# A new instruction order for a one-core attention and PReLU kernel: every step at a new place, fill matmuls regrouped, alpha's loads behind a GpSimd step

## The chip, the cores and the metric

The kernel runs on one core of a Trainium2 chip. A core has a matrix engine (TensorE, "PE" in the profile; its weight loads are listed apart as "PEld"), a vector engine (VectorE, "DVE"), an activation engine (ScalarE, "ACT"), a general engine (GpSimd, "POOL") and a queue engine (SyncE, "SP"). Each engine runs its own list of instructions in order; engines wait for one another through semaphores. A DMA (a copy between main memory and the core's memory SBUF, or a transposing copy) is issued as an instruction of SP, ACT or POOL and runs beside the engines once issued. TensorE writes into PSUM, eight banks of 2 KB per partition that VectorE and ScalarE read out.

The metric is the device time of one execution in microseconds (us), the median of several runs.

## The reference, cut to what matters

There are eight batches of eight heads, 512 tokens of width 64, and 32 states per head. Tokens read the states and the states read the tokens, both through a softmax; what was read goes, heads joined to a row of 512, through a two-layer network with a PReLU whose slope `alpha` differs for each of the 2048 hidden columns.

```python
scores = x @ state.T / 8                     # per batch and head
xread  = softmax(scores, over states) @ state        # (512, 64)
sread  = softmax(scores.T, over tokens) @ x          # (32, 64)
rows   = heads joined of concat([xread, sread])      # (8 * 544, 512)
h = rows @ w_in                                      # (4352, 2048)
g = maximum(h, 0) + alpha * minimum(h, 0)
out = g @ w_out                                      # (4352, 512)
```

## The kernel before, in words

**An order written out.** The kernel's steps are small functions. A string `ORDER` (line 18) names them one after the other with their arguments, and the loop at line 767 calls them in that order, under a manual schedule: nothing is reordered afterwards. So the order of the string is the order of the instructions on each engine and each queue; semaphores for true dependences and for the reuse of buffers are put in by the framework. A token is `step.arguments`. The last argument, where it is a letter, is the engine that does the copy: `a` ScalarE, `v` VectorE, `p` GpSimd.

**Stages.** For each batch b the steps are:

- `lx` (line 160) loads x of the batch in 16 bits by a DMA that POOL issues, into one of three buffers `xg`; `xd` (291) issues on SP the transposing DMA that writes `xT`. Batches 0 and 1 are transposed on TensorE instead (`xt` 299, with the copy `xo` 304), and batch 0 is loaded on SP in 32 bits and cast (`cx` 176), so that it can start early. The states come by `lst` (203), and are transposed on TensorE (`stt`, `sto`, `sbd`, `str`, `sro`, lines 244 to 282).
- `sc` (314) makes the scores, into a pair of PSUM banks called `two` of which there is one. From it follow two softmaxes. Over the states: `sb` (346, VectorE transposes 32x32 blocks), `smax` (379), `ssh` (384), `sexp` (393, ScalarE), `ssum` (402), `snorm` (406), `wb` (414, transposes back into `aT`). Over the tokens: `tm` (426), `nb` (433), `te` (443, ScalarE), `tsum` (453), `tn` (459 or 461), `tt` (465, a transposing DMA on SP into `e2T`). For batch 0 the state softmax works on scores of its own (`tsc` 353, in two halves) and `at`/`ao` (365, 368) transposes back on TensorE.
- `m` (507) multiplies the states by a quarter f of `w_in`, which makes the weights of the first layer directly from the states (the attention and `w_in` are one matrix then); `mo` (531, 533) copies the result to SBUF.
- `F` (556) is the first layer for one of 16 groups of 128 hidden columns: two matmuls into one bank, 512 tokens wide. `N` (609, ScalarE) takes the negative part out of that bank, `G` (612, VectorE) joins both to g; only then is the bank free. In batch 0 some of these come by halves of the tokens: `f`, `n`, `g` (578, 593, 597).
- In batch 0 `S` (626) is the second layer, in eight steps of two matmuls for each quarter of the tokens, and `O` (644) its output. From batch 1 on the second layer is done by seven products of half blocks instead of eight (a Winograd form of Strassen's scheme): `W` (670, GpSimd) makes differences of `w_out` once, `U` (694, GpSimd) makes sums and differences of g, `P` (715) are the products, four matmuls each, into the banks `px`, `py`, `pv`; `K` (731) keeps intermediate sums in SBUF, and `Q` (746, 748) makes and stores one quarter of the output, by an addition on VectorE or a copy on ScalarE, and a DMA on SP. Its buffer `osb` exists four times.
- `rd` (480) reads the tokens by the states' softmax, 32 small matmuls from `xg` and `e2T`; `rdo` copies the result. What all batches' states read is "batch 8", run at the end: its `F` is line 565.

**Weights.** `wi` (212) and `wo` (218) load quarters of `w_in` and `w_out` through POOL, with a cast. As POOL issues these DMAs itself, each is also 0.7 to 1.0 us of POOL's time. `W`, `U`, `tn` on POOL, `lx` and `lst` stand in the same queue.

**Fills.** `Z.k.n` (236) are n matmuls of a pattern into bank k which nobody reads; the setup does sixteen of them at the very start (`fill(0, 16)`).

**Banks.** Six banks are given out by number: the last digit of an `F`, and of the first `S` or `P` of a bank, is the bank 0 to 5 it takes. A step that takes a bank waits until its former content was read.

**alpha.** Before the loop the setup clears `alpha_rows` on VectorE (line 186) and issues its four loads on SP (188), behind the two loads of batch 0's x. `oma` (272, 273) turns it by a VectorE transpose and makes 1 - alpha on ScalarE, which every `G` and `g` needs.

Of the kernel before, what the change touches and what calls it, by code (L numbers as in the profile page):

```python
# [18 lines left out]
Z.0.3 stc.a stt.0 cx.0.1.v xt.0.0.1.1 xo.0.0.1.a wi.0 cx.0.0.v xt.0.0.0.2 xo.0.0.0.a sbd.0.v lst sbd.1.v Z.3.2 sto.a  # L19
Z.3.2 Z.3.3 cx.1.0.v xt.0.1.0.3 cx.1.1.v tsc.0.1.4 tsc.0.0 smax.0.0 ssh.v.0.0 xo.0.1.0.a xt.0.1.1.5 xo.0.1.1.a Z.1.3  # L20
Z.1.2 sc.0.0 sc.0.1 tsc.1.1.1 m.0.0.2.0 tsc.1.0 sexp.0.0 tm.0 smax.0.1 ssum.0.0 Z.3.3 mo.0.0.a.1 lx.1 Z.3.2 Z.3.2
Z.3.3 ssh.v.0.1 str.1.3 nb.0.a te.0.1 Z.5.3 str.0.5 Z.4.3 Z.4.3 te.0.0 sexp.0.1 Z.4.2 mo.0.0.v.0 Z.4.3 wi.1 ssum.0.1
wo.0 sro.0.a xt.1.0.0.4 snorm.p.0.0 at.0.0 ao.0.a wo.1 Z.1.3 tsum.0 snorm.p.0.1 xt.1.0.1.1 m.1.0 xt.1.1.0.2 sro.1.a
wi.2 oma.a xo.1.0.0.v wi.3 xo.1.0.1.v xo.1.1.0.a f.0.0.0.5 xt.1.1.1.0 n.0.0.0 mo.1.0.v at.1.4 ao.1.v m.0.1.1.3
tn.0.1.p mo.0.1.v.1 m.1.1 mo.1.1.a g.0.0.0.0 g.0.0.0.1 f.0.0.1.2 n.0.0.1 f.0.1.1.4 mo.0.1.a.0 n.0.1.1 f.0.1.0.3
xo.1.1.1.v g.0.0.1.1 g.0.0.1.0 sc.1 tm.1 m.2.0.5.0 mo.2.0.a.1 mo.2.0.a.0 F.0.5.1 N.0.5 F.0.4.2 N.0.4 nb.1.a te.1.1
g.0.1.1.0 g.0.1.1.1 G.0.5 S.0.3.0.0 wo.2 G.0.4 S.0.1.0.5 S.0.1.1 sb.1 F.0.7.4 N.0.7 G.0.7 F.0.6.1 wo.3 tn.0.0.p N.0.6
S.0.3.1 G.0.6 n.0.1.0 g.0.1.0.0 S.0.2.2.2 S.0.3.2 te.1.0 S.0.1.2 S.0.2.0 g.0.1.0.1 m.0.2 S.0.2.3 S.0.1.3 smax.1
mo.0.2.a F.0.8.4 N.0.8 G.0.8 W.1.1.p F.0.11.1 N.0.11 G.0.11 tsum.1 F.0.10.3 N.0.10 m.0.3 mo.0.3.a W.1.0.p lx.2 S.0.2.1
S.0.3.3 F.0.9.4 m.1.2 F.0.12.1 ssh.p.1 sexp.1 G.0.10 S.0.2.5 S.0.1.5 ssum.1.s N.0.9 G.0.9 F.0.13.3 S.0.3.5 mo.1.2.a  # L30
m.1.3 N.0.12 G.0.12 S.0.3.4 F.0.15.4 tn.1.1.a N.0.13 G.0.13 F.0.14.1 S.0.1.4 S.0.3.6 S.0.1.6 W.2.0.p S.0.2.4 N.0.15
snorm.p.1 wb.1 F.1.3.3 G.0.15 S.0.2.6 F.1.7.4 tn.1.0.a W.2.1.p N.0.14 G.0.14 mo.1.3.a N.1.3 G.1.3 N.1.7 G.1.7 xd.2
tt.0 S.0.3.7 O.0.3.a F.1.12.1 N.1.12 G.1.12 F.1.1.3 N.1.1 W.4.1.p F.1.9.0 G.1.1 N.1.9 G.1.9 tt.1 S.0.2.7 O.0.2.a
F.1.2.4 N.1.2 G.1.2 F.1.10.1 N.1.10 S.0.1.7 sc.2 O.0.1.a tm.2 sb.2 m.2.2.3.2 mo.2.2.a.0 W.4.0.p rd.0.0 G.1.10
mo.2.2.a.1 F.1.0.4 N.1.0 rdo.0.a W.3.1.p lx.3 S.0.0.6.5 nb.2.a F.1.8.3 N.1.8 G.1.0 smax.2 te.2.0 F.1.4.2 S.0.0.7 G.1.8
te.2.1 F.1.5.0 N.1.5 S.0.0.5 G.1.5 F.1.11.1 N.1.11 S.0.0.2 S.0.0.4 S.0.0.3 G.1.11 N.1.4 G.1.4 m.2.1 mo.2.1.a F.1.6.4
N.1.6 G.1.6 F.1.15.3 N.1.15 G.1.15 F.1.13.0 N.1.13 S.0.0.0 F.1.14.1 N.1.14 W.3.0.p S.0.0.1 O.0.0.a ssh.p.2 sexp.2 xd.3
U.1.1.0.p G.1.13 P.1.1.0.1.2 P.1.1.1.1 m.3.2 m.2.3.4.3 mo.2.3.a.1 mo.2.3.a.0 G.1.14 m.3.0.5.0 ssum.2.1 P.1.1.0.0
U.1.2.0.p mo.3.0.a.0 P.1.1.1.0 K.1.1.a P.1.2.0.0.3 snorm.v.2 wb.2 P.1.2.1.0 P.1.2.0.1 U.1.1.1.p U.1.2.1.p P.1.2.1.1
mo.3.2.a P.1.6.1.0 mo.3.0.a.1 m.3.3.4.5 mo.3.3.a.1 mo.3.3.a.0 rd.1.1 Q.1.0.0 sc.3 tm.3 m.4.0.0.5 mo.4.0.a.0 sb.3  # L40
P.1.6.0.0 mo.4.0.a.1 rdo.1.a F.2.6.4 N.2.6 G.2.6 F.2.13.3 N.2.13 P.1.6.0.1 P.1.6.1.1 F.2.0.0 F.2.12.5 F.2.8.1 G.2.13
K.1.2.a P.1.5.1.0 N.2.0 N.2.12 G.2.12 G.2.0 P.1.5.1.1 P.1.5.0.0 N.2.8 G.2.8 nb.3.a te.3.0 F.2.2.4 N.2.2 G.2.2 te.3.1
# [12 lines left out]
F.3.11.0 N.3.11 P.2.3.0.1 G.3.11 F.3.5.5 N.3.5 P.2.3.1.1 U.3.3.0.p P.2.3.0.0 G.3.5 mo.5.3.a.1 sexp.4 U.3.1.1.p
m.7.0.3.0 sc.5 P.2.3.1.0 Q.2.0.1.a mo.7.0.a.1 mo.7.0.a.0 tm.5 P.2.2.1.0.2 ssum.4.5 P.2.2.0.1 P.2.2.0.0 m.7.3.4.0
mo.7.3.a.1 mo.7.3.a.0 P.2.4.0.1 P.3.2.0.0.3 P.2.2.1.1 nb.5.a te.5.1 te.5.0 P.2.4.1.0 P.2.4.0.0 P.3.2.1.0 P.2.4.1.1
tsum.4 tn.4.0.a tn.4.1.a tt.4 P.3.2.0.1 snorm.v.4 wb.4 F.4.11.0 N.4.11 F.4.13.4 P.3.1.0.0.5 P.3.1.0.1 Q.2.1.0 sb.5
G.4.11 Q.2.0.0 xd.6 P.3.1.1.1 N.4.13 G.4.13 F.4.4.1 N.4.4 U.3.1.0.p G.4.4 U.3.2.0.p P.3.2.1.1 P.3.1.1.0 smax.5 K.3.1.a
Q.3.0.0 F.4.10.0 m.6.1.2.4 N.4.10 mo.6.1.a.1 mo.6.1.a.0 G.4.10 U.3.2.1.p m.5.1 P.3.6.1.0 tsum.5 F.4.5.1 N.4.5 G.4.5  # L60
U.3.3.1.p F.4.9.4 N.4.9 F.4.1.2 N.4.1 G.4.9 F.4.2.3 P.3.6.0.0 F.4.14.0 P.3.6.1.1 F.4.15.1 G.4.1 N.4.2 N.4.14 U.3.4.0.p
ssh.p.5 U.3.4.1.p G.4.2 mo.5.1.a G.4.14 N.4.15 P.3.7.1.0.4 G.4.15 F.4.3.2 P.3.7.0.0 N.4.3 G.4.3 P.3.6.0.1 K.3.2.a
F.4.0.3 N.4.0 sc.6 sb.6 rd.4.0 rdo.4.a m.7.2.1.2 P.3.5.1.0 mo.7.2.a.1 P.3.5.0.1 F.4.8.0 N.4.8 sexp.5 lx.7 tm.6 G.4.0
smax.6 mo.7.2.a.0 G.4.8 F.4.12.2 P.3.5.0.0 P.3.5.1.1 K.3.4.a F.4.7.3 ssh.p.6 N.4.7 N.4.12 P.3.7.1.1 P.3.7.0.1 Q.3.1.1
F.4.6.1 P.3.3.1.0 P.4.1.1.0.0 nb.6.a te.6.1 P.3.4.1.0 G.4.7 P.3.3.0.0 P.3.3.0.1 G.4.12 P.4.2.1.1.3 P.4.2.0.1 P.4.1.0.0
P.3.3.1.1 P.3.4.1.1 N.4.6 sexp.6 ssum.5.2 G.4.6 P.4.1.0.1 Q.3.0.1.a P.3.4.0.0 m.6.2.1.5 P.3.4.0.1 te.6.0 P.4.2.0.0
# [36 lines left out]
def kernel(  # L103
# [26 lines left out]
    n_jc = d_ff // 128  # L130
# [56 lines left out]
    for q in range(4):  # L187
        nc.sync.dma_start(
            alpha_rows[N * q : N * q + n_jc, :],
            moe_alpha.rearrange("(jc q p) -> q jc p", q=4, p=N)[q],  # L190
        )
# [608 lines left out]
```

## Time and profile before

| | |
|---|---|
| median of 3 runs | 214.46 us (214.04 to 214.86) |
| the profiled execution | 214.07 us |
| its span, from the first instruction to the last | 212.0 us |
| granted TensorE clock | 1.0 |
| TensorE busy | 203.3 us, 96% of the span |
| GpSimd busy | 179.1 us, 84% |
| VectorE busy | 174.2 us, 82% |
| ScalarE busy | 152.6 us, 72% |
| DMA | 23.70 MB, mean 112 GB/s |

A row of the timeline reads: start in us, duration in us, engine, line, operation, tile written <- tiles read, shape, number of instructions in the row; in brackets how long the engine had been idle before, and what ended that. Rows of the chain of waits are start, duration, engine, tile and line, count. Rows of groups are line, engine, operation, tiles, count | busy us in total, mean ns of one | idle us before them, and what ended most of it. Rows of the waits are who waited <- for whom: us in total, times, longest us. The strips of digits show the span in 40 equal slices of 5.3 us, busy share in tenths.

### The profile page before, as it was taken

To read this page: it belongs to the slowest core of one execution; us is meant where nothing else is said; L and a number is where in the kernel's file an instruction comes from. 1 tells how busy PE (TensorE), PEld (TensorE's weight loads), DVE (VectorE), ACT (ScalarE), POOL (GpSimd) and SP (SyncE) were. 2 spreads that over 40 slices of the span, in tenths; PEclk is the share of its full clock that TensorE was granted. 3 is DMA by queue.
4 is the path that set the end of the run, shared out by engine and by line. 5 is a ranking of instruction groups with operands and counts; after the bars stand their busy time and mean duration, and the time that the engine had idled before them with its cause. 6 is when DMAs were issued, how large, how long until landed. Compare 5 with 4: busy or idle time off the path is not lost.

```text
span 212.0 us, 5108 instructions
## 1 busy us (share of the span) xinstructions
PE 203.3 (96%) x2034; PEld 137.7 (65%) x2034; DVE 174.2 (82%) x260; ACT 152.6 (72%) x300; POOL 179.1 (84%) x111
## 2 busy tenths in 40 slices
PE   7899999999999999999999998999999999999991
PEld 4556333444666665677667875667688777888880
DVE  0787988999999999999999999898999777654340
ACT  2577979999999999999797777887954584234100
POOL 8048848998999899999996999479996999999860
PEclk9999999999999999999999999999999999999999
DMA  6999995966665436778744539011521201111232
GB/s 159 219 204 207 206 204 89 160 165 90 152 105 89 106 84 135 110 134 143 183 117 49 103 106 192 3 51 40 162 53 49 99 3 49 49 53 49 74 124 102
DMA packets 43975, 23.70 MB, mean 112 GB/s; under 512 B 22192, under 2 KB 43440, under 8 KB 43952
## 3 DMA queue, kind: packets, MB, share of 16 engines
q1 hardware_dynamic: 31904, 15.22, 27.9%
q0 software_dynamic: 11776, 8.09, 26.6%
q8 instruction: 16, 0.26, 0.5%
q10 hardware_dynamic: 272, 0.07, 0.1%
q14 instruction: 7, 0.06, 0.1%
HBM read 17.31 MB, written 8.91 MB: 124 GB/s over the span
## 4 chain that ended last, share of the span: by engine, by line
PE 88%; DMA 7%; ACT 2%; issue 1%; SPq 0%; DVE 0%; ACTq 0%
PE h L556 25%; PE px L715 23%; PE pv L715 12%; PE o L626 6%; PE py L715 5%; PE m_ps L507 4%; PE h L565 3%; PE fill L236 3%; DMA xT<-xg 2%; DMA x<-in_x_dram 2%; PE sr_ps L480 2%; DMA out_dram<-oq 2%; DMA e2T<-e 1%; PE sc L314 1%; PE xT_ps L299 1%; PE h L578 1%
## 5 line engine op out<-in xcount | busy, mean ns | idle before, releaser
L612 DVE SCALAR_TENSOR_TENSOR g<-neg,oma_sb,h 128x512 f16<-128x512 f32 (+1 forms) x140 | 92.7, 708 | 11.6 <-ACT neg L609 11.1
L609 ACT ACTIVATE neg<-h 128x512 f32<-128x512 f32 (+1 forms) x140 | 75.0, 585 | 23.0 <-PE h L556 14.4
L556 PE MATMUL h<-aT,m 128*128 128x512 f16 x248 | 67.2, 379 | 0.1
L715 PEld LDWEIGHTS <-gsum 128*128 128x128 f16 x480 | 46.1, 98 | 16.8 <-issue 1.8
L715 PEld LDWEIGHTS <-g 128*128 128x128 f16 x360 | 35.0, 98 | 9.1 <-issue 0.9
L694 POOL TENSOR_TENSOR gsum<-g 128x1024 f16<-128x1024 f16 (+1 forms) x16 | 32.0, 2009 | 4.2 <-DVE g L612 3.6
L694 POOL TENSOR_TENSOR gsum<-g,g 128x1024 f16<-128x1024 f16 (+1 forms) x16 | 32.0, 2004 | 3.9 <-DVE g L612 3.8
L556 PEld LDWEIGHTS <-m 128*128 128x128 f16 x248 | 23.7, 98 | 15.5 <-issue 0.8
L694 POOL TENSOR_TENSOR gsum<-gsum,g 128x1024 f16<-128x1024 f16 (+1 forms) x16 | 32.1, 2006 | 1.1
L715 PE MATMUL px<-ws,gsum 128*128 128x256 f16 x240 | 32.6, 273 | 0.0
L694 POOL TENSOR_TENSOR gsum<-g,gsum 128x1024 f16<-128x1024 f16 (+1 forms) x16 | 31.9, 2005 | 0.1
L731 ACT COPY kept<-px 128x512 f32<-128x512 f32 (+1 forms) x22 | 12.7, 577 | 14.0 <-PE px L715 13.7
L533 ACT CAST m<-m_ps 128x512 f16<-128x512 f32 x36 | 20.0, 613 | 1.8 <-PE m_ps L507 1.5
L384 POOL TENSOR_TENSOR ts<-ts,mx 128x1024 f32<-128x1024 f32 x7 | 13.4, 1908 | 5.4 <-DVE mx L379 5.4
L715 PE MATMUL px<-w_out_sb,gsum 128*128 128x256 f16 x120 | 17.4, 273 | 0.0
L715 PE MATMUL pv<-ws,gsum 128*128 128x256 f16 x120 | 17.2, 273 | 0.0
L748 DVE TENSOR_TENSOR oq<-pv,kept 128x512 f32<-128x512 f32 (+1 forms) x16 | 10.5, 655 | 8.1 <-PE pv L715 6.7
L626 PE MATMUL o<-w_out_sb,g 128*128 128x512 f16 x64 | 17.1, 380 | 0.0
L715 PE MATMUL pv<-ws,g 128*128 128x256 f16 x120 | 16.9, 273 | 0.0
L715 PE MATMUL px<-w_out_sb,g 128*128 128x256 f16 x120 | 16.9, 273 | 0.0
L715 PE MATMUL py<-w_out_sb,g 128*128 128x256 f16 x120 | 16.2, 273 | 0.0
L531 ACT CAST m<-m_ps 128x1024 f16<-128x1024 f32 x12 | 12.4, 1032 | 1.3 <-PE m_ps L507 1.2
(76 smaller groups left out, 251.6 us busy)
## 6 DMA issues: line engine op xcount, KB each, us to landing
out_dram<-oq SPq DMA_DIRECT2D x28, 256.0 KB, 2.5
xg<-in_x_dram POOLq DMA_DIRECT2D x7, 512.0 KB, 6.9
w_in_sb<-in_moe_w_in_dram POOLq DMA_DIRECT2D x4, 512.0 KB, 9.3
w_out_sb<-in_moe_w_out_dram POOLq DMA_DIRECT2D x4, 512.0 KB, 12.2
x<-in_x_dram SPq DMA_DIRECT2D x2, 512.0 KB, 5.3
out_dram<-osb SPq DMA_DIRECT2D x4, 256.0 KB, 2.2
out_dram<-oq SPq DMA_DIRECT2D x4, 128.0 KB, 2.1
st<-in_state_dram POOLq DMA_DIRECT2D x1, 224.0 KB, 8.0
```

What stands on the lines that cost most here:

```text
L384: engine(e).tensor_tensor(blocks(cols(live["ts", b], j, S)), blocks(scored(b, j)), over_blocks(cols(live["mx", b], j, S // N)), ALU.subtract,)
L507: nc.tensor.matmul(t[N * k : N * (k + 1), :], st_head(b, h)[64 * r : 64 * r + 64, :], w_in_sb[64 * r : 64 * r + 64, c, 512 * f : 512 * (f ...
L531: copier(e)(m_tile(b, f), t)
L533: copier(e)(m_tile(b, f)[:, g, :], t[g])
L556: nc.tensor.matmul(h.rearrange("p (r j s) -> p r j s", r=2, j=2), ms[b, f][:, g, 128 * j : 128 * (j + 1)], weights(b, g), start=(g == 0), ...
L609: nc.scalar.activation(neg, h, RELU, bias=0.0, scale=-1.0)
L612: nc.vector.scalar_tensor_tensor(g_tile(b, jc), negs.pop((b, jc)), oma_sb[:, jc : jc + 1], hs.pop((b, jc)), ALU.mult, ALU.add,)
L626: nc.tensor.matmul(outs[b, q], g_tile(b, jc)[:, 128 * q : 128 * (q + 1)], w_out_sb[:, jc, :], start=not begun and jc == 2 * jc2, stop=left ...
L694: engine(e).tensor_tensor(t, x(), y(), op)
L715: nc.tensor.matmul(pbanks[b, name][:, i, :], of(b, c)[:, j, 128 * i : 128 * (i + 1)], moving[:, 4 * c + j, :], start=not begun and j == 0, ...
L731: copier(e)(t, pbanks[b, "x"])
L748: nc.vector.tensor_tensor(osb, pbanks[b, name], kept[b, add], ALU.add)
```

## The change

Two things change. The whole string `ORDER` is replaced by another, of 1109 tokens instead of 1117; and alpha's loading becomes a step.

The new string holds the same steps of computation: each engine's work is the same list of operations in another order, except where the letter of a copying step changed. Seven operations fewer are on ScalarE and five more on VectorE (five more of `mo`, two `K`, two `xo` and one `sto` there, fewer `cx`, `sbd` and one `Q`), and two `tn` moved to GpSimd. Numbers of banks changed with the order. The fill matmuls between the steps, 42 in both, come in seven groups of 9, 3, 3, 9, 6, 6 and 6 instead of sixteen of two or three. TensorE has 2034 matmuls in both.

`alpha_rows` is now cleared by GpSimd, and its four loads on SP are issued with it in the step `la`, which stands behind `sexp.0.0`; on GpSimd the step comes behind `wi.0`, `lst`, `lx.1` and `wi.1`, and the loads wait for the clearing.

The start of both strings, and places in the middle that the prediction speaks of (cut):

```diff
-Z.0.3 stc.a stt.0 cx.0.1.v xt.0.0.1.1 xo.0.0.1.a wi.0 cx.0.0.v xt.0.0.0.2 xo.0.0.0.a sbd.0.v lst sbd.1.v Z.3.2 sto.a
-Z.3.2 Z.3.3 cx.1.0.v xt.0.1.0.3 cx.1.1.v tsc.0.1.4 tsc.0.0 smax.0.0 ssh.v.0.0 xo.0.1.0.a xt.0.1.1.5 xo.0.1.1.a Z.1.3
-Z.1.2 sc.0.0 sc.0.1 tsc.1.1.1 m.0.0.2.0 tsc.1.0 sexp.0.0 tm.0 smax.0.1 ssum.0.0 Z.3.3 mo.0.0.a.1 lx.1 Z.3.2 Z.3.2
...
-xo.1.1.1.v g.0.0.1.1 g.0.0.1.0 sc.1 tm.1 m.2.0.5.0 mo.2.0.a.1 mo.2.0.a.0 F.0.5.1 N.0.5 F.0.4.2 N.0.4 nb.1.a te.1.1
-g.0.1.1.0 g.0.1.1.1 G.0.5 S.0.3.0.0 wo.2 G.0.4 S.0.1.0.5 S.0.1.1 sb.1 F.0.7.4 N.0.7 G.0.7 F.0.6.1 wo.3 tn.0.0.p N.0.6
...
-F.1.2.4 N.1.2 G.1.2 F.1.10.1 N.1.10 S.0.1.7 sc.2 O.0.1.a tm.2 sb.2 m.2.2.3.2 mo.2.2.a.0 W.4.0.p rd.0.0 G.1.10
-mo.2.2.a.1 F.1.0.4 N.1.0 rdo.0.a W.3.1.p lx.3 S.0.0.6.5 nb.2.a F.1.8.3 N.1.8 G.1.0 smax.2 te.2.0 F.1.4.2 S.0.0.7 G.1.8
...
-mo.3.2.a P.1.6.1.0 mo.3.0.a.1 m.3.3.4.5 mo.3.3.a.1 mo.3.3.a.0 rd.1.1 Q.1.0.0 sc.3 tm.3 m.4.0.0.5 mo.4.0.a.0 sb.3
...
-U.4.2.0.p U.4.1.1.p U.4.2.1.p tn.5.1.p Q.4.0.0 P.4.6.1.0 F.5.8.4 P.4.6.0.0 xd.7 N.5.7 G.5.7 snorm.v.6 N.5.10 G.5.10
...
-F.5.1.5 N.5.1 G.5.1 P.4.5.0.1 P.4.5.0.0 F.5.6.3 N.5.6 P.4.5.1.1 G.5.6 P.4.5.1.0 tt.5 m.7.1.1.2 rd.5.4 mo.7.1.a.0 sc.7
...
-F.6.3.5 G.6.1 P.5.5.0.0 P.5.5.0.1 rd.6.1 tt.7 rd.7.2 rdo.7.a P.5.5.1.1 P.5.7.0.0 P.5.5.1.0 P.5.7.0.1 G.6.10 K.5.4.a
...
-P.8.4.0.0 Q.8.0.0 Q.8.1.0 P.8.3.0.1 Q.8.0.1.a
...
+stc.a stt.0 cx.0.1.a sbd.1.a sbd.0.a cx.0.0.v xt.0.0.0.1 xt.0.0.1.2 Z.3.9 xo.0.0.0.v wi.0 cx.1.1.v xt.0.1.1.3 lst
+xo.0.0.1.a sto.v tsc.0.0.4 lx.1 wi.1 xo.0.1.1.v cx.1.0.a tsc.0.1 xt.0.1.0.5 smax.0.0 Z.1.3 xo.0.1.0.a ssh.v.0.0 sc.0.0
+sexp.0.0 la sc.0.1 tm.0 m.0.0.1.2 mo.0.0.a.1 ssum.0.0 tsc.1.0.0 snorm.p.0.0 wo.0 wi.2 nb.0.a te.0.1 tsc.1.1 smax.0.1
...
+xo.1.0.1.v wo.2 mo.2.0.v.1 f.0.1.0.0 n.0.1.0 Z.2.6 xo.1.1.0.v m.1.1 mo.1.1.v mo.2.0.a.0 m.0.1.2.4 at.1.1 Z.5.6
...
+F.0.4.0 Z.3.6 tm.1 sb.1 g.0.0.1.0 g.0.0.1.1 nb.1.a f.0.0.0.3 smax.1 S.0.3.0.5 g.0.1.1.0 g.0.1.1.1 N.0.4 G.0.4 te.1.1
...
+F.1.10.0 N.1.10 F.1.7.4 N.1.7 G.1.11 sc.2 sb.2 tm.2 smax.2 G.1.10 O.0.3.a W.2.1.p rd.0.3 lx.3 xd.3 rdo.0.a rd.1.1
...
+m.3.3.4.5 mo.3.3.a.1 wb.2 m.5.0.2.3 mo.5.0.a.1 sc.3 P.1.1.1.0 F.2.15.1 F.2.0.5 mo.5.0.a.0 F.2.3.3 mo.3.3.a.0 N.2.0
...
+U.3.1.0.p P.3.1.0.0 U.3.2.0.p K.3.1.a P.3.2.0.0.0 ssh.p.5 U.3.1.1.p U.3.2.1.p P.3.2.0.1 P.3.2.1.1 P.3.2.1.0 Q.3.0.0
...
+P.3.7.0.1 P.3.5.1.1 P.3.5.1.0 te.6.0 m.7.0.5.2 xd.7 m.6.3.0.3 P.3.7.1.0 mo.6.3.a.1 tsum.5 P.3.7.0.0 F.4.0.3 mo.7.0.a.0
+mo.7.0.a.1 wb.5 P.3.5.0.0 sb.6 N.4.0 P.3.5.0.1 mo.6.3.v.0 F.5.15.5 G.4.0 K.3.4.a Q.3.1.1 F.5.2.2 N.5.2 F.4.10.0 N.4.10
...
+te.6.1 tt.5 N.4.8 G.4.8 N.5.15 G.5.15 F.5.4.2 N.5.4 G.5.4 U.4.3.0.p F.5.8.0 P.3.3.1.0 P.3.4.1.0 N.5.8 G.5.8 F.4.7.3
...
+ssh.p.6 mo.7.1.a.1 U.4.1.0.p F.5.5.0 N.5.5 nb.7.a tsum.6 F.5.10.3 N.5.10 mo.7.1.v.0 U.4.1.1.p U.4.2.0.p U.4.2.1.p
...
+P.4.4.0.0 snorm.v.6 wb.6 P.4.4.0.1 F.6.6.5 G.5.1 Q.4.1.0 tt.7 G.5.9 F.6.11.0 F.6.12.4 P.4.3.0.1 ssh.p.7 P.5.1.0.1.1
...
+U.8.3.1.p P.8.7.0.1 Q.8.1.1 U.8.4.1.p P.8.3.0.1 U.8.4.0.p P.8.3.0.0 Q.8.0.1.v P.8.4.0.0 P.8.4.0.1 Q.8.1.0
```
```diff
 alpha_rows = consts.tile([128, N], F32)
-nc.vector.memset(alpha_rows, 0.0)
-for q in range(4):
-    nc.sync.dma_start(
-        alpha_rows[N * q : N * q + n_jc, :],
-        moe_alpha.rearrange("(jc q p) -> q jc p", q=4, p=N)[q],
-    )
 alpha_sb = consts.tile([128, N], F32)
+
+def load_alpha():
+    nc.gpsimd.memset(alpha_rows, 0.0)
+    for q in range(4):
+        nc.sync.dma_start(
+            alpha_rows[N * q : N * q + n_jc, :],
+            moe_alpha.rearrange("(jc q p) -> q jc p", q=4, p=N)[q],
+        )
...
 steps = {
...
+    "la": load_alpha,
```

## The prediction

> **What bounds the kernel now.** I read the page first (shares, slices, chain), then TensorE's waits, the chain in order of time, and the timeline of the start.
>
> ```profile
> span 212.0 us, 5108 instructions
> ...
> PE 203.3 (96%) x2034; PEld 137.7 (65%) x2034; DVE 174.2 (82%) x260; ACT 152.6 (72%) x300; POOL 179.1 (84%) x111
> ...
> DVE  0787988999999999999999999898999777654340
> ...
> PEclk9999999999999999999999999999999999999999
> ...
> PE 88%; DMA 7%; ACT 2%; issue 1%; SPq 0%; DVE 0%; ACTq 0%
> ```
> ```profile
> PE sr_ps L480 <- DMA e2T<-e: 1.0, 1, 1.0
> ...
> PE sc L314 <- DMA xT<-xg: 0.4, 1, 0.4
> ```
>
> TensorE is the bound: 88% of the chain, and after the start only two waits of note. VectorE is second: nine tenths or more in every slice (of 5.3 us) from 37 to 132 us.
>
> So I count with one quantity. Both orders hold the same TensorE steps, so for any step I take its start and subtract the priced work of all real steps (fills not counted) ahead of it. What is left is the time lost so far, and the kernel whose loss is larger at the end is slower. Prices come from the chain in order of time, where steps stand back to back:
>
> ```profile
> 35.80 0.86 PE h L556 x4
> ...
> 60.38 0.87 PE px L715 x8
> ...
> 72.55 0.55 PE m_ps L507 x16
> ...
> 129.30 2.85 DMA e2T<-e
> 132.29 0.68 PE sr_ps L480 x32
> ```
>
> An F is two matmuls, 0.43 us; an S the same (same shape); a P four, 0.44; an rd all 32, 0.68; an m eight, 0.27. All real steps together come to 187 us: 25 of the 212.0 are lost, 4.5 of them after the last matmul. Three places before, from the timeline:
>
> ```profile
> 22.81 1.76 PE L626 MATMUL o<-w_out_sb,g 128*128 128x512 f16 x6
> ```
> ```profile
> 44.27 0.60 PE L556 MATMUL h<-aT,m 128*128 128x512 f16 x2
> ```
> ```profile
> 206.91 0.60 PE L715 MATMUL px<-w_out_sb,gsum 128*128 128x256 f16 x4
> ...
> 208.18 0.37 ACT L746 COPY oq<-px 128x256 f32<-128x256 f32 x1 [2.88 <-DMA out_dram<-oq]
> ```
>
> S.0.3.0 at 22.81 has 8.3 us ahead: 14.5 lost. F.1.0 at 44.27 has 28.2 ahead: 16.1. The last P at 206.91 has 186.5: 20.4. More than two thirds of the loss is made in the first 23 us; the rest is small change, the 0.4 and 1.0 of the two waits in it.
>
> **The change part by part.** *Fills.* Their sum is 42 in both orders beside the sixteen of the setup (16 groups before, 7 after), so nothing is left out in total.
>
> ```profile
> 1.24 3.85 PE L236 MATMUL fill<-pattern 128*128 128x256 f16 x19 [1.24 <-POOL pattern L194]
> ```
> ```profile
> 14.15 2.02 PE L236 MATMUL fill<-pattern 128*128 128x256 f16 x11
> ```
>
> The eleven fills at 14.15 are four groups; at 0.11 us each (a P's matmul has the same 256 columns) they need 1.2 of the 2.02, so a group costs some 0.2 besides. Nine groups fewer free 1.8 us of TensorE, worth nothing while VectorE is late there (next).
>
> *The start, moved steps.* VectorE's own rows give its spacing, start to start:
>
> ```profile
> 10.09 1.23 DVE L426 TENSOR_REDUCE nb<-sc 128x2 f32<-128x1024 f32 x1
> 11.23 0.68 DVE L379 TENSOR_REDUCE mx<-tsc 128x16 f32<-128x512 f32 x1
> 11.83 0.68 DVE L402 TENSOR_REDUCE r<-ts 128x16 f32<-128x512 f32 x1
> ...
> 12.71 0.63 DVE L384 TENSOR_TENSOR ts<-tsc,mx 128x512 f32<-128x512 f32 x1
> ...
> 16.66 0.42 DVE L304 COPY xT<-xT_ps 128x512 f16<-128x512 f16 x1 [1.51 <-PE xT_ps L299]
> ...
> 18.02 1.23 DVE L531 CAST m<-m_ps 128x1024 f16<-128x1024 f32 x1
> ...
> 19.58 0.69 DVE L533 CAST m<-m_ps 128x512 f16<-128x512 f32 x1
> 20.18 0.86 DVE L597 SCALAR_TENSOR_TENSOR g<-neg,oma_sb,h 128x256 f16<-128x256 f32 x2
> ```
> ```profile
> 41.33 2.72 DVE L612 SCALAR_TENSOR_TENSOR g<-neg,oma_sb,h 128x512 f16<-128x512 f32 x4 [0.23 <-ACT neg L609]
> 43.97 1.22 DVE L426 TENSOR_REDUCE nb<-sc 128x2 f32<-128x1024 f32 x1
> 45.10 1.24 DVE L346 STREAM_TRANSPOSE ts<-sc 128x1024 f32<-128x1024 f32 x1
> 46.27 1.36 DVE L612 SCALAR_TENSOR_TENSOR g<-neg,oma_sb,h 128x512 f16<-128x512 f32 x2
> 47.55 1.21 DVE L379 TENSOR_REDUCE mx<-ts 128x32 f32<-128x1024 f32 x1
> ```
> ```profile
> L612 DVE SCALAR_TENSOR_TENSOR g<-neg,oma_sb,h 128x512 f16<-128x512 f32 (+1 forms) x140 | 92.7, 708 | 11.6 <-ACT neg L609 11.1
> ```
>
> The first loads are the same, so smax.0.0 starts near 8.6, as the first maximum before. From there the new order gives VectorE, without a gap: smax, ssh, tm, ssum, smax, ssh (0.6, 0.6, 1.1, 0.9, 0.6, 0.6), mo 0.6, ao 0.4 (as an xo), two small steps 0.3, xo 0.4, ssum 0.9, xo 0.4, mo 0.6, xo 0.4: 8.4 us, to 17.0. The softmax part is earlier than before (the 1.51 us of idling at 16.66 are gone), but mo.1.1 now needs w_in's second quarter:
>
> ```profile
> 4.22 0.78 POOL L212 DMA_DIRECT2D w_in_sb<-in_moe_w_in_dram  x1
> ```
> ```profile
> DMA to landing us min/median/max: 7.8/9.3/12.7
> ```
>
> Issued at 4.22, with the longest of that line's landings (12.7), it is there at 16.9; with its matmuls mo.1.1 runs at 17.4 for 1.2; then two g 0.8, tm.1 and sb.1 (1.1 and 1.2), two g 0.8, smax.1 1.2, two g 0.8 and waits of a few tenths put the end of g.0.1.1.1 at 24.6 (the sum alone gives 23.5; I add the 1.1 that the same stretch idled before by waits for ACT). It frees the bank of S.0.1.0, which has 9.1 us ahead: 15.5 lost, **1.0 more** than before. Then 22 G at 0.66, two g, ssum.1 and tsum.1 1.6, wb.1 1.2 (as sb), sb.2, tm.2 and smax.2 3.4, and 0.9 of waiting for N.0.6: 22.4 us, so G.1.10 ends at 47.0. F.1.0 writes the bank that it frees, with 29.4 ahead: 17.6 lost, **1.5 more** (the 1.0 included). Before, G.1.10 stood in front of smax.2, and F.1.0 was not held. Bounds: 0.5 if w_in lands a microsecond sooner; 2.6 if each of the 22 G costs the 0.71 that one lasts in the mean (last row, a group of the page) instead of 0.66, the spacing of the four at 41.33.
>
> *From 47 to 104 us.* After G.1.10 VectorE has 41 G, 5 Q, two mo, an rdo and three rounds of softmax, in all 53.8 us to G.4.4; before it was 44 G, 6 Q, an rdo and the same softmax, 55.2. That keeps G.4.4 near 103, just ahead of F.4.9 which needs its bank: no term, up to 1.0 if it slips. The 0.4 us at sc.3 goes, since lx.3 is issued before W.4.1 and xd.3 can leave at 50: **minus 0.4** (0 if xd.3 finds SP taken).
>
> *The transposes.*
>
> ```profile
> 116.98 9.32 SPq L749 DMA_DIRECT2D out_dram<-oq  x4
> 126.41 2.79 SPq L291 DMA_TRANSPOSE xT<-xg  x1
> 129.30 1.28 SPq L465 DMA_TRANSPOSE e2T<-e  x1
> ```
>
> Before, xd.7 stands behind four outputs on SP's queue, the last waiting for Q.4.0.0, and tt.5 behind xd.7; rd.5 waits for it. After, xd.7 is behind Q.3.0.0 and tt.5 behind Q.3.1.1, some 20 and 2 us ahead of need: **minus 1.1** (0 if Q.3.1.1 is late). Late next is tt.7, now behind Q.4.1.0: from the product's end an addition (0.7), the output's issue (0.6) and 2.85 of transpose, with semaphores 4.8 us, and 5.2 us of products stand between.
>
> *GpSimd.* Two more tn, the memset and the moved queue places are within its idle time. Its sums take 2.1 us each:
>
> ```profile
> L694 POOL TENSOR_TENSOR gsum<-gsum,g 128x1024 f16<-128x1024 f16 x14 | 29.8, 2128 | 0.9
> ```
>
> U.4.1.0 to U.4.4.0 are seven behind ssh.6, which waits for smax.6 at about 121.5; with 2.0 for ssh.6 they end at 138.1, when P.4.3.0 needs the last of them. For this and tt.7 I take **plus 0.5** (bounds 0 and 2.1, one whole sum).
>
> *alpha.* The loads leave at 5.1, behind GpSimd's fourth load and a memset, and are needed at 14.3.
>
> ```profile
> 1.90 2.89 SPq L188 DMA_DIRECT2D alpha_rows<-in_moe_alpha_dram  x4
> ```
> ```profile
> DMA to landing us min/median/max: 4.5/4.9/6.4
> ```
>
> With the same issue time and the longest landing they are there at 14.4 at worst. No cost; up to 0.5. No gain either: what SP's queue carries next comes later than this in both orders.
>
> *The end.* Before, the last copy waited until 208.18 for an output buffer, 0.67 after the last matmul. After, that buffer's earlier output leaves nine products before the end, and the last step is an addition: **minus 0.4** (0 to minus 0.7).
>
> Sum: 1.5 − 0.4 − 1.1 + 0.5 − 0.4 = 0.1 us. The profiled execution took 214.07 us; the median of three runs is 214.46, 0.4 more. So 214.2 beside the profiled one, and as a median 214.5 (rounded down).
>
> **The rivals.** *Faster:* VectorE keeps up, so the 1.5 shrinks to 0.5 and the 0.5 of new waits to nothing: 0.1 − 1.5 = −1.4, 213.1; with a microsecond of the 1.8 that the fills free, 212.1. For it: the 1.51 us of VectorE's idling at 16.66 close. Against: tm, sb and smax of batches 1 and 2 now stand in a row, 3.4 us in which no bank is freed.
> *Slower, VectorE becomes the bound from 14 to 104 us.* Price: 0.71 for 0.66 (22 times, 1.1 us) at the start, and as the 41 later ones cost it too, the 1.0 at G.4.4: 0.1 + 2.1 = 2.2, 216.7; with one late sum (2.1 for the 0.5) it would be 218.3. It decides from 0.04 us per G on (1.0 us in 22). For it: the slices of nine tenths, and five mo, two K and three copies more than before on an engine that is never ahead. Against: the spacing in the rows at 41.33 and 46.27.
> *Slower, by the clock.* The sixteen and three fills at 1.24 took 3.85 us where warm ones need 2.1 (19 at 0.11): a spell at half speed. The fills that went leave TensorE some 70% occupied from 13 to 25 us, its longest pause 1.2 us. One more such spell costs up to 1.8 us, so 216.3. Against: no later row shows it, and the granted clock stands at nine tenths or more in every slice. The Trainium skill, "TensorE: Matmul & The Clock Gate", Part 1, has the clock halved after an idle window of about 3.4 us; by that rule pauses of 1.2 us would not bring it about.
> *Slower, by a transpose:* Q.4.1.0 a microsecond late or two put rd.7 and all behind it back by as much: 215.5 to 216.5.
>
> **Chances.** No change 0.38, faster 0.27, VectorE 0.25, transposes and sums 0.07, clock 0.03. 0.5% is 1.07 us, about what a measurement of this kernel tells from none. The likeliest case has its own range, 213.4 to 215.5; with the faster and the VectorE case it is 212.0 to 217.5. The slower cases lie beyond the 0.5%: faster 0.27, same 0.38, slower 0.35.
>
> **What would show it.** Right: S.0.1.0 at 24.5 to 25, VectorE without gaps over 0.6 us from 9 to 45; F.1.0 at 47; no wait of rd.5 on e2T; less than 0.1 us between the last product and its addition. Wrong: S.0.1.0 before 24 or after 25.5; TensorE waiting on G between 50 and 104 us; GpSimd sums or e2T as releasers of TensorE after 110; matmuls of 0.2 us instead of 0.11 in the start.

## The result, and the profile after

The new order takes 216.05 us in the median (17 executions, 214.69 to 217.57), the kernel before 214.40 (214.01 to 214.88): a ratio of 1.0074, with a 95% interval of 1.0051 to 1.0097. It is slower by 1.6 us, outside the half per cent within which I had called "no change" the likeliest, and inside the range of 212.0 to 217.5. Two things stand out: the executions spread over 2.9 us where the kernel before spreads over 0.9, and the profiled one (215.0, span 213.2) is among the quick ones. One profile therefore shows less than the whole loss.

The page of the new order; shares, slices and chain, as shown of before:

```profile
span 213.2 us, 5109 instructions
...
PE 201.7 (95%) x2034; PEld 137.3 (64%) x2034; DVE 176.6 (83%) x264; ACT 148.9 (70%) x293; POOL 180.8 (85%) x114
...
DVE  0799989897899999999999999999799885525441
...
PE 63%; DMA 14%; POOL 11%; DVE 8%; issue 2%; ACT 1%; POOLq 0%; DVEq 0%
```

Work per engine is as good as unchanged, but the chain that ended last runs over TensorE for 63% instead of 88%; transfers have doubled to 14%, and GpSimd and VectorE, at nothing or nearly so before, hold 19%. The waits of TensorE name the places (who waited <- for whom: us in total, times, longest):

```profile
PE h L558 <- DVE g L614: 1.7, 2, 1.3
PE o L628 <- DVE g L599: 1.3, 1, 1.3
...
PE sc L316 <- DMA xT<-xg: 0.7, 1, 0.7
...
PE sr_ps L482 <- DMA e2T<-e: 0.4, 1, 0.4
```

The wait of rd.5 on e2T (1.0 us before) is gone, one of 0.4 for rd.7 has come. In their places, from the timeline of the new order:

```profile
24.22 0.61 PE L628 MATMUL o<-w_out_sb,g 128*128 128x512 f16 x2 [1.30 <-DVE g L599]
```
```profile
47.62 0.59 PE L558 MATMUL h<-aT,m 128*128 128x512 f16 x2 [1.32 <-DVE g L614]
```
```profile
57.81 0.41 PE L316 MATMUL sc<-xT,stT 64*32 64x256 f16 x16 [0.73 <-DMA xT<-xg]
```
```profile
148.09 0.68 PE L482 MATMUL sr_ps<-e2T,xg 128*64 128x32 f16 x32 [0.35 <-DMA e2T<-e]
```
```profile
208.08 1.04 PE L717 MATMUL pv<-ws,g 128*128 128x256 f16 x8
```

With the prediction's own measure (start less priced work ahead), in us: S.0.1.0 at 24.22 has 9.1 ahead, 15.1 lost; F.1.0 at 47.62 has 29.4, 18.2 lost; sc.3 at 57.81 has 38.2, 19.6 lost; rd.7 at 148.09 has 126.3, 21.8; the last two products at 208.08 have 186.1, 22.0. At the end that is 1.6 more than the 20.4 of before; the tail behind the last matmul is 0.4 shorter (209.1 to 213.2, before 207.5 to 212.0), and 1.2 remains, the difference of the spans. The other 0.4 to 0.5 of the 1.6 in the medians, and the spread, are not in this execution.

The chain in order of time shows why sc.3 waited (start, duration, what):

```profile
43.83 6.55 DMA xg<-in_x_dram
...
50.39 7.38 DMA xT<-xg
...
57.81 0.41 PE sc L316 x16
```

and the same step before:

```profile
53.51 4.79 DMA xT<-xg
```

The transpose xd.3 leaves SP at 50.39, as predicted, and then takes 7.38 us instead of 4.79. GpSimd issues the next load, lx.4, just behind it:

```profile
50.92 0.92 POOL L159 DMA_DIRECT2D xg<-in_x_dram  x1
```

Before, lx.4 left at 59.4, after xd.3 had landed. Five theories follow for the 1.6 us and the spread. **Theory 1:** xd.3 is stretched by lx.4's load, as the transfers share the DMA engines. **Theory 2:** VectorE's new order (the row at 47.62) is the loss. **Theory 3:** VectorE stands behind w_in's second quarter, whose landing varies. **Theory 4:** the block of nine fills. **Theory 5:** alpha's place.

### The profile page after: what moved, and what is told of

Same layout as the page of the kernel before. It is cut to its first block, busy times and chain, and to the rows that moved or that the text cites. A ratio compares the mean times of both kernels' runs of the same rounds, so it can differ in the third digit from the quotient of the medians.

```text
span 213.2 us, 5109 instructions
## 1 busy us (share of the span) xinstructions
PE 201.7 (95%) x2034; PEld 137.3 (64%) x2034; DVE 176.6 (83%) x264; ACT 148.9 (70%) x293; POOL 180.8 (85%) x114
## 4 chain that ended last, share of the span: by engine, by line
PE 63%; DMA 14%; POOL 11%; DVE 8%; issue 2%; ACT 1%; POOLq 0%; DVEq 0%
PE px L717 20%; PE h L558 18%; PE pv L717 10%; POOL gsum L696 7%; DMA w_in_sb<-in_moe_w_in_dram 6%; PE py L717 5%; DMA xT<-xg 3%; PE h L567 3%; DMA xg<-in_x_dram 3%; DVE g L614 3%; PE m_ps L509 2%; POOL ts L386 2%; PE o L628 2%; DMA e2T<-e 2%; PE sr_ps L482 1%
## 5 line engine op out<-in xcount | busy, mean ns | idle before, releaser
L558 PE MATMUL h<-aT,m 128*128 128x512 f16 x248 | 66.4, 379 | 1.7 <-DVE g L614 1.7
L535 ACT CAST m<-m_ps 128x512 f16<-128x512 f32 x31 | 17.2, 595 | 2.2 <-PE m_ps L509 1.8
L717 PE MATMUL px<-w_out_sb,g 128*128 128x256 f16 x120 | 17.5, 273 | 0.0
L717 PE MATMUL pv<-ws,gsum 128*128 128x256 f16 x120 | 16.7, 273 | 0.0
L717 PE MATMUL px<-w_out_sb,gsum 128*128 128x256 f16 x120 | 16.4, 273 | 0.0
L717 PE MATMUL pv<-ws,g 128*128 128x256 f16 x120 | 16.1, 273 | 0.0
L733 ACT COPY kept<-px 128x512 f32<-128x512 f32 (+1 forms) x20 | 11.7, 583 | 4.5 <-PE px L717 4.4
```

What stands on the lines that cost most here:

```text
L535: copier(e)(m_tile(b, f)[:, g, :], t[g])
L558: nc.tensor.matmul(h.rearrange("p (r j s) -> p r j s", r=2, j=2), ms[b, f][:, g, 128 * j : 128 * (j + 1)], weights(b, g), start=(g == 0), ...
L717: nc.tensor.matmul(pbanks[b, name][:, i, :], of(b, c)[:, j, 128 * i : 128 * (i + 1)], moving[:, 4 * c + j, :], start=not begun and j == 0, ...
L733: copier(e)(t, pbanks[b, "x"])
```

## The experiments

**Alpha back at the start.**

```diff
-    def load_alpha():
-        nc.gpsimd.memset(alpha_rows, 0.0)
+    nc.vector.memset(alpha_rows, 0.0)
+    for q in range(4): nc.sync.dma_start(...)
...
-sexp.0.0 la sc.0.1
+sexp.0.0 sc.0.1
```

> The new order, alpha cleared and loaded at the start as before. If alpha's place costs nothing (my reading: landed at 10.9, needed at 14.1 in the trace of after), the time stays that of the new order, 216.0 within its spread of some 0.5, and F.1.0 still starts at about 47.6. If the later loads do cost (DMA traffic shifted onto w_in's second quarter), the time falls by 0.5 or more and m.1.1 starts before 16.

215.84 us (214.43 to 217.43), ratio to before 1.0078 (1.0046 to 1.011): as the new order. Theory 5 falls. But in its profiled execution (217.43, its slowest) m.1.1 came at 18.1, where the new order has it at 16.7, and the reason is the most useful row of the study. In the timeline of this kernel the first block of nine fills:

```profile
6.68 2.12 PE L235 MATMUL fill<-pattern 128*128 128x256 f16 x9
```

and in that of the new order, the same instructions:

```profile
6.47 1.15 PE L238 MATMUL fill<-pattern 128*128 128x256 f16 x9
```

0.24 us for one instead of 0.13. TensorE ran at half speed, as it does in the setup's fills at 1.24 (3.59 us for the sixteen), and all that follows came 1.4 us later. The Trainium skill, "TensorE: Matmul & The Clock Gate", Part 1, says that the window by which the clock is released runs free and does not start with the kernel, so that one kernel finds a different number of slow matmuls from run to run. The two rows are in line with it; no run here shows the window itself. In this execution xd.3 took even longer:

```profile
51.98 8.20 DMA xT<-xg
```

**mo.1.1 on ScalarE.**

```diff
-m.1.1 mo.1.1.v
+m.1.1 mo.1.1.a
```

> The new order with the copy mo.1.1 on ScalarE instead of VectorE, so VectorE does not stand behind w_in's second quarter. Theory 'the start is lost by VectorE waiting for w_in': g.0.1.1.1 ends up to 1.2 us earlier, S.0.1.0 starts near 23 instead of 24.2, and the run-to-run spread (2.9 us) shrinks; time 215.0 to 215.4. Theory 'the bank order at G.1.10 decides': VectorE only waits a little more elsewhere, F.1.0 still starts after 47, time within 0.4 of 216.0.

217.06 us (216.22 to 219.33), ratio 1.0152 (1.0113 to 1.019): slower than the new order, which neither theory expected. S.0.1.0 starts at 24.8, not at 23. The wait for w_in has only changed engines. In this kernel's timeline TensorE now stands behind ScalarE, which stands behind the quarter of w_in and has the copies of two banks behind it:

```profile
18.48 0.82 PE L238 MATMUL fill<-pattern 128*128 128x256 f16 x6 [1.08 <-ACT m L535]
```

Theory 3 falls in this form: VectorE's wait for w_in was 0.5 us in the trace of the new order, and with VectorE out of that wait the spread is still 3.1 us.

**G.1.10 in front of the softmax of batch 2.**

```diff
-G.1.11 sc.2 sb.2 tm.2 smax.2 G.1.10
+G.1.11 G.1.10 sc.2 sb.2 tm.2 smax.2
```

> The new order with G.1.10 in front of sc.2, sb.2, tm.2 and smax.2 on VectorE. Theory 'bank order': F.1.0 starts 3 us earlier at most, its wait of 1.3 us is gone, but sc.3's wait on xT keeps a part: time 0.9 to 1.5 lower, 214.5 to 215.1. Theory 'VectorE is the bound': the next G is late by as much, the wait goes to another F, time within 0.4 of 216.0.

215.44 us in the median of twelve (212.97 to 218.27). The ratio of 1.0023 (0.9993 to 1.0053) leaves out the two longest, 217.30 and 218.27; the median of the other ten is 214.87, 1.2 below the new order and inside the 0.9 to 1.5 expected. The lowest time fell by 1.7, from 214.69 to 212.97. F.1.0 starts at 46.06 without a wait:

```profile
46.06 0.59 PE L558 MATMUL h<-aT,m 128*128 128x512 f16 x2
...
47.48 0.81 PE L628 MATMUL o<-w_out_sb,g 128*128 128x512 f16 x3 [0.39 <-ACT XS L493]
```

So the bank order costs about what was put on it (Theory 2 is right so far), and something else, changing from execution to execution, lies on top: the ten still spread over 3.1 us. F.1.0 comes 1.6 us earlier; 0.4 of it goes into the wait in the second row, and the span is 0.8 shorter. VectorE is not the bound here.

**lx.4 behind two sums.**

```diff
-... U.1.3.1.p ... lx.4 ... G.1.2 mo.2.3.a.0 xd.4 ... U.1.1.0.p U.1.2.0.p U.1.1.1.p
+... U.1.3.1.p ... G.1.2 U.1.1.0.p U.1.2.0.p lx.4 mo.2.3.a.0 xd.4 ... U.1.1.1.p
```

> The new order with the load lx.4 behind two GpSimd sums, so that it does not run beside the transpose xd.3. Theory 'contention': xd.3 takes some 4.8 us as before instead of 7.4, sc.3 does not wait for xT, time 0.7 to 0.9 lower, about 215.2. Theory 'slow by itself': xd.3 still takes 6 us or more and the time stays at 216.0 within 0.4.

214.15 us (213.73 to 215.81), ratio 1.0008 (0.9993 to 1.0024). This one move takes back the loss, more than the 0.7 to 0.9 expected, and most of the spread: eleven of twelve executions lie within 1.1 us. xd.3 leaves at 50.50 and lands after 4.26 us, with no other transfer in flight; lx.4 leaves only then, and sc.3 runs behind the work in front of it without a wait for xT:

```profile
50.50 1.96 SPq L293 DMA_TRANSPOSE xT<-xg  x1
...
56.27 0.92 POOL L159 DMA_DIRECT2D xg<-in_x_dram  x1
...
56.59 0.62 PE L509 MATMUL m_ps<-w_in_sb,stT 64*32 64x512 f16 x16
57.03 0.40 PE L316 MATMUL sc<-xT,stT 64*32 64x256 f16 x16
```

Theory 1 holds, and this is the "no change" of the forecast: in the median all of the new order but lx.4's place is worth nothing against the kernel before. (The two sums that pass lx.4 are moved by the same edit.)

**lx.4 earlier.**

```diff
-ssh.p.2 U.1.3.1.p te.2.1
+ssh.p.2 lx.4 U.1.3.1.p te.2.1
```

> The new order with the load lx.4 two places earlier on GpSimd, issued some 1.5 us before xd.3 instead of 0.5 after. Theory 'contention': the whole of xd.3 runs beside the load, it takes 8 us or more, sc.3 waits longer and the time is 216.5 to 218. Theory 'chance, not lx.4': as the new order, 216.0 within 0.4, and xd.3 between 6 and 8 us.

214.99 us (214.38 to 215.94, 8 executions), ratio 1.0033 (1.0013 to 1.0054): better than the new order, and my expectation was wrong. lx.4 left 2.2 us ahead of xd.3 and had landed at 56.1; xd.3 took 5.8. So an overlap alone does not give the price: a load issued well ahead stretches the transpose less than one issued just behind it. Over the profiles, xd.3 by the time from its own issue to lx.4's:

| kernel | lx.4 issued after xd.3, us | xd.3, us |
|---|---|---|
| alpha_start | 0.3 | 8.20 |
| after_fill0 (below) | 0.4 | 7.79 |
| mo11_act | 0.5 | 7.86 |
| the new order | 0.5 | 7.38 |
| g110_first | 1.0 | 6.36 |
| lx4_early | −2.2 | 5.78 |
| before | 5.9 | 4.79 |
| lx4_late | 5.8 | 4.26 |

A difference of 0.7 us in when GpSimd comes to its load moves the transpose by 1.8. In the last two rows the load leaves after the transpose has landed; before, an output of 256 KB was in flight beside it. The eight executions fall in two groups, 214.38 to 214.50 and 215.47 to 215.94; the profiled one, of the upper group, has slow fills again:

```profile
6.67 2.12 PE L238 MATMUL fill<-pattern 128*128 128x256 f16 x9
```

**No fills between the steps.** The kernel is lx4_late.

```diff
-(Z.3.9 Z.1.3 Z.3.3 Z.4.9 Z.2.6 Z.5.6 Z.3.6)
```

> lx4_late without any of the 42 fill matmuls between the steps (the sixteen of the setup stay). If fills only pass time in which TensorE waits, 214.15 within 0.3, or 0.2 lower. If they keep TensorE's speed up, matmuls of some stretch before 25 us last twice as long, and the time is 0.5 to 2 us above lx4_late.

214.06 us (213.46 to 214.90), ratio 0.9995 (0.998 to 1.0011): the same as with them. But of the other case that the expectation names, the first half came true. Without the fills TensorE does run slow in stretches before 25 us, at a granted clock of 0.78 in the mean from 10 to 15 us where the new order has 1.00. The 28 transposes of the states, without the fills and then with them (lx4_late):

```profile
10.49 1.70 PE L249 MATMUL st_ps<-ident,st 128*64 128x128 f16 x28
```
```profile
11.05 0.97 PE L250 MATMUL st_ps<-ident,st 128*64 128x128 f16 x28 [0.28 <-DMA st<-in_state_dram]
```

So the fills do keep TensorE's speed up, and in this order that is worth nothing in the median: S.0.1.0 starts at 24.2 there, behind a G of VectorE as with them.

**The three moves together.** lx.4 late, G.1.10 first, and the transpose of batch 7 in front of an output:

```diff
-G.5.1 Q.4.1.0 tt.7 G.5.9
+G.5.1 tt.7 Q.4.1.0 G.5.9
```

> The new order with three moves together: lx.4 behind two GpSimd sums, G.1.10 in front of sc.2, and the transpose tt.7 in front of Q.4.1.0. If the three losses are separate (F.1.0 1.3 to 1.6 us, xd.3 the contention, rd.7 0.4), the time is that of lx4_late less 1.3 to 2.0: 212.2 to 212.9, below the kernel before (214.2), with a spread under 1.2 us. If VectorE is the bound from 25 to 60 us, the gain at F.1.0 comes back at sc.3 or at a later G, and the time is 213.6 to 214.2.

213.06 us (212.46 to 214.90), ratio 0.9950 (0.9928 to 0.9971). The gains add to those of lx4_late, 1.1 in the median (lowest against lowest 1.3), a little under the 1.3 to 2.0 expected: rd.7's and F.1.0's waits are gone. (The wait of 0.3 us on a G that is left stands at an earlier F, at 33.8; the new order has it too, at 31.6.) Seven executions lie at 212.46 to 213.26 and five at 213.84 to 214.90, so a second source of spread is still in. The profiled one, of the upper five, had quick fills (1.15 us) and another mishap, in its waits of TensorE: a load of x that landed 1.2 us later than in the others.

```profile
PE xT_ps L301 <- DMA xg<-in_x_dram: 1.4, 1, 1.4
```

**Where it comes from: the combo with a colder start.**

```diff
-    fill(0, 16)
+    fill(0, 6)
```

> The combo with six instead of sixteen fills in the setup, so that TensorE idles from about 2.5 to 5.2 us and comes cold to the nine fills at 6.5. Theory 'cold block': the nine take 2.1 us in every execution and not only in some, all that follows is 1.1 to 1.4 us late: median 213.9 to 214.3 with few executions below 213.5. Theory 'late executions come from transfers': as combo, 213.06 within 0.3, the lowest near 212.5.

214.01 us (213.74 to 214.74, twelve executions), ratio 0.9992 (0.9981 to 1.0003). No execution comes near the 212.5 of the combo any more, and none is far above: the cost is made in all of them. The profile:

```profile
1.25 1.46 PE L238 MATMUL fill<-pattern 128*128 128x256 f16 x6 [1.25 <-POOL pattern L196]
...
6.73 2.13 PE L238 MATMUL fill<-pattern 128*128 128x256 f16 x9
```

From the lowest to the lowest that is 1.3 us, of which the nine fills make 1.0.

**The combo with Z.0.3 back.**

```diff
+Z.0.3
 stc.a stt.0 ...
-Z.3.9
+Z.3.6
```

> The combo with the three fills Z.0.3 put back in front of stc, as in the kernel before, and six instead of nine in Z.3. If the block of nine behind a gap of TensorE at 5 us is what makes some executions late (in the profile of alpha_start these nine took 2.12 us instead of 1.15), executions over 1 us above the median vanish, the median stays that of combo within 0.3. If the late executions come from transfers, both the median and the spread stay.

212.84 us in the median of five executions, 212.56 to 213.86, ratio 0.9937 (0.9917 to 0.9956); a sixth took 724 us and is left out (single ones of the kernel before took 238 to 528). Four of the five lie within 0.32. That points the expected way, on few executions.

**The same fills in the kernel before.**

```diff
-Z.0.3 stc.a ...
+stc.a ...
-Z.3.2 sto.a Z.3.2 Z.3.3
+Z.3.9 sto.a
```

> The kernel before with its first fills regrouped as the new order has them: Z.0.3 left out in front of stc, and one Z.3.9 in place of Z.3.2, Z.3.2 and Z.3.3. If the cold block of nine is what spreads the executions, some of them (about a quarter) take 0.5 to 1.4 us more than 214.3 and the spread grows from 0.9 to 1.5 or more. If the order before has room for it (VectorE idles 1.5 us at 16.7), median and spread stay at 214.3 and 0.9.

214.06 us (213.54 to 215.97), ratio 1.0005 (0.9982 to 1.0028). Nine of twelve lie at 213.54 to 214.17, a little below the kernel before, and three at 215.33 to 215.97: a quarter, as expected. So the regrouped fills alone bring executions 1.5 us late into an order that had none (but for three single ones above 237 us, no execution of the kernel before took longer than 214.94). Its profiled execution (213.87) is of the lower group, with nine fills in 1.15 us, so slow fills are not shown in a late one of this kernel.

**The new order with only the fills put back**, Z.0.3 in front and six instead of nine, lx.4 beside xd.3.

> The new order with one edit: the three fills Z.0.3 back in front of stc and six instead of nine in the first Z.3; lx.4 stays beside xd.3. The 17 times of the new order fall into 214.7 to 215.7 and 216.0 to 217.6. If the upper part is the cold block, it goes: median 215.0 to 215.4, highest below 216.2, and what is left above 214.15 (lx4_late) is the contention of xd.3, about 1.0 us. If the upper part is the contention, both parts stay and the median is 216.0 within 0.4.

215.20 us (ten of eleven at 214.23 to 215.67, one at 218.28, which the ratio leaves out), ratio 1.004 (1.0025 to 1.0054). The upper half of the new order's times is gone but for that one; what is left above lx4_late is 1.05 us in the medians, and the profile shows it at the transpose:

```profile
PE sc L316 <- DMA xT<-xg: 1.3, 1, 1.3
```

**One more move**, on combo_fill0:

```diff
-smax.1 S.0.3.0.5 g.0.1.1.0 g.0.1.1.1 N.0.4
+S.0.3.0.5 g.0.1.1.0 g.0.1.1.1 smax.1 N.0.4
```

> combo_fill0 with smax.1 behind g.0.1.1.0 and g.0.1.1.1 on VectorE. S.0.1.0's wait of 1.3 us falls by about 1.1. If TensorE is the bound there, the time falls by 0.6 to 1.1, to 211.8 to 212.3. If VectorE is the bound from 25 to 46 us, F.1.0's wait of 0.3 grows by as much and the time stays at 212.86 within 0.3.

211.90 us (211.84 to 212.19, four executions), ratio 0.9891 (0.9876 to 0.9907): below both kernels, by 2.4 us against the one before. S.0.1.0 starts at 22.91 instead of 24.28. Of these 1.4 us a new wait takes 0.8 back, and the 0.3 at a later F is gone:

```profile
22.91 0.60 PE L628 MATMUL o<-w_out_sb,g 128*128 128x512 f16 x2 [0.18 <-DVE g L599]
...
24.69 0.59 PE L558 MATMUL h<-aT,m 128*128 128x512 f16 x2 [0.84 <-DVE g L614]
```

F.1.0 and the end come 0.9 to 1.0 earlier. VectorE is close to being the bound in these 25 us, and is not yet. That F.1.0 had a wait of 0.3 left, as the expectation says, was a misreading: the wait stood at the earlier F.

## Why the prediction was right or wrong, point by point

*The time and its range.* 216.05 lies outside the 213.4 to 215.5 of the likeliest case and inside 212.0 to 217.5. That width was kept for the case in which VectorE becomes the bound, and that case did not come, so the range held by luck. What came, a stretched transpose and slow matmuls, stood under names that had 0.07 and 0.03.

*The measure* held: the lost time at the end, 22.0 against 20.4 and a tail 0.4 shorter, is the difference of the two profiled spans.

*The start.* smax.0.0 at 8.53 (predicted 8.6), mo.1.1 at 17.20 (17.4), w_in landed at 16.7 (16.9), g.0.1.1.1 out at 24.16 (24.6), S.0.1.0 at 24.2: 0.6 more lost than before, where I had 1.0. F.1.0 at 47.62 (47.0): 2.1 more instead of 1.5, since VectorE waited for ScalarE 1.06 us at N.0.6 and 0.49 at a later N, where I had 0.9 in all, and its 22 G cost 0.68 each instead of 0.66 (timeline of the new order):

```profile
27.27 0.75 DVE L614 SCALAR_TENSOR_TENSOR g<-neg,oma_sb,h 128x512 f16<-128x512 f32 x1 [1.06 <-ACT neg L611]
...
38.64 4.88 DVE L614 SCALAR_TENSOR_TENSOR g<-neg,oma_sb,h 128x512 f16<-128x512 f32 x7 [0.49 <-ACT neg L611]
```

The mechanism, G.1.10 behind three reductions, was right, and g110_first shows its price.

*"The 0.4 us at sc.3 goes", minus 0.4:* this is the step that failed. I took xd.3's leaving time, which was right to 0.4 us, and gave it the duration that it had before. I had named "0 if xd.3 finds SP taken" as the bound; SP was free. What I did not ask is what else moves data then: rd.1 comes right after rd.0 in the new order, so the buffer of lx.4 is free early, and GpSimd issues it half a microsecond behind xd.3. In the profiled execution the term is plus 0.4 (19.6 − 18.2 against 17.1 − 16.1), and by after_fill0 against lx4_late 1.05 us in the median. The Trainium skill, "DMA: Bandwidth & Descriptors", "Issuing engines are not separate DMA queues", says that transfers started by SP and by GpSimd run on the same engines and interleave; the table above agrees, with 4.3 us alone and up to 8.2 beside a load. That the load's place is the cause is shown: in lx4_late and the kernels built on it the load leaves after xd.3 has landed, and xd.3 takes 4.26 to 4.51 us. How the two transfers hold each other up is not shown.

*Fills, at nothing.* This failed too. For the median of a quick execution it is right (lx4_nofill). But I counted groups and their time, and weighed the clock only between 13 and 25 us, at 0.03 and with the granted clock as evidence. The place was the first block: without Z.0.3, TensorE sometimes reaches the nine fills slow, and each of the nine then costs twice as much, in front of batch 0's second half. That is 1.0 us in the fills and 1.3 to 1.4 in all that follows, and by after_fill0 0.85 in the median (216.05 to 215.20). The argument that pauses of 1.2 us would not bring a slow spell about does not hold either: in lx4_nofill the 28 transposes ran slow, and the longest pause of TensorE behind the setup's fills had been 1.14 us by then.

*The transposes.* rd.5's wait went (1.0 in the row of before, 1.1 in the sum); tt.7 became the late one and costs 0.4, as bounded in the 0.5. *GpSimd's sums* ended at 138.87 (138.1) and P.4.3.0 did not wait. *alpha* landed at 10.9, no cost. *The end:* minus 0.4, as predicted. *47 to 104 us:* no wait on a G behind F.1.0, as predicted. *The signs:* rd.5 and the last addition (0.04 us behind its product) came as for right, and F.1.0 nearly; S.0.1.0 at 24.2 fell between the two. VectorE's gap of 1.06, a wait on e2T at 148 and, in the profiles of alpha_start and lx4_early, matmuls of 0.2 us in the start came as for wrong.

With lx.4 out of the way the time is 214.15 (lx4_late), where 214.2 to 214.5 had been forecast. That close an agreement is in part luck: F.1.0 still loses 0.6 more than the sum had, and the span of lx4_late's profile is 0.7 above that of before, not 0.1. What stands above 214.15, 1.9 us, is by after_fill0 about 1.05 of a stretched transpose and 0.85 of slow fills (0.95 and 0.8, if each is taken against the kernel before as measured beside it). Of the rivals, "VectorE becomes the bound" did not come as the loss (lx4_late took all of it back with VectorE's order as it was), "by a transpose" named the wrong one, and "by the clock" was right in kind and wrong in place.

Open: how often a start is slow, and so how the 1.9 us between the new order and lx4_late divide. Of the eight profiles of kernels with sixteen fills in the setup and the block of nine, two had the slow fills. Late executions were nine of seventeen in the new order, three of twelve in before_z9 and only one of twelve in lx4_late, whose start is that of the new order. By after_fill0 the transpose is 1.05 and the start 0.85; by lx4_late alone the transfer would be all of it. The two may also not be separate: in alpha_start, with the slow start, lx.4 came closer behind xd.3 (0.3 us instead of 0.5), xd.3 took 0.8 longer and sc.3 waited 1.8 instead of 0.7. And the late start of the combo's profile shows that not every late execution is the fills'.

## What to carry to other kernels

When a step's transfer moves, list what else is in flight in its new place, and not only which queue it stands in: here one load, issued half a microsecond behind a transpose on the critical path, cost 1 us. Look at the spread beside the median: here a tripled spread with unchanged work was the sign that something hung on a landing time or on TensorE's speed, and a single profile showed only one draw of it. Filler work in front of the first real work has a price that doubles when TensorE is slow: nine fills in one block cost 1 us more in such executions.

## What the runs showed of the hardware

A transpose of one batch (SBUF to SBUF) takes 4.3 us alone and 6.4 to 8.2 us beside a 512 KB load from GpSimd issued 0.3 to 1.0 us behind it. It is not only such loads: in g110_first the next transpose, xd.4, took 6.04 us with no load in flight, beside two outputs of 256 KB issued 2 and 3 us behind it. Nine matmuls of 256 columns took 1.15 us or 2.12 us at the same point of programs that start alike (the new order and lx4_early). The granted clock in the profile did not tell the two apart, though it did tell of the slow stretch of lx4_nofill at 10 us. In the windows of alpha_start (columns: window, its length, busy time of the engines, granted clock, DMA share, GB/s) it stands at 1.00 while the nine slow fills run:

```profile
6.60:8.80 2.20, 2.20 (x12) 1.40 (x11) 0.94 (x3) 1.25 (x3) 0.00 (x0) 1.00 1.30 207
```

Taking that row of nines as evidence that the clock was up, as I had done, is not safe in the first microseconds; the duration of one matmul is.
